# Seven half-size products in place of eight for the output product of the last batch

## The chip, the cores and the metric

The kernel runs on one core of one Trainium2 chip. The metric is the device time of one execution in microseconds. Before the change it is 569.72 us, the median of three runs (569.68 to 569.75).

## What is computed

Two stages follow one another. The first is an attention across channels for each of four batches of 5824 tokens with 256 channels; the second is a gated feed-forward layer over all 23296 tokens.

```
qn = q / (norm(q, over tokens) + 1e-6);  kn = k / (norm(k, over tokens) + 1e-6)
s  = kn^T @ qn / tau                      # 256 x 256 for each batch
a  = softmax(s, last axis)
x  = v @ a                                # tokens x 256
out = (((x @ w1) * (x @ w2)) @ w3) @ w_out    # d_ff = 1024, output tokens x 256, float32
```

Nothing nonlinear stands between `v @ a` and `w1`, `w2`, nor between `w3` and `w_out`. The kernel uses both facts: for each batch it folds `a` into `w1` and `w2` (called Wf, 256 x 1024 twice), and it multiplies `w3` by `w_out` once (called W_sb, 1024 x 256). What remains for each token is v times Wf twice, an elementwise product, and that product times W_sb.

## The kernel before, in words

A batch has 45 blocks of 128 tokens and 64 tokens left over. The main loop runs over the batch b (4), the chunk c (12) and the step j (8). Chunks 0 to 10 hold 512 tokens each; chunk 11 holds 128 tokens and the 64 left over, 192 columns. Step j stands for 128 of the 1024 hidden columns.

One step does this. `emit_ab` (L476) issues four matmuls, two for `a` and two for `b`, each 128 hidden columns by 512 tokens, into two tiles of PSUM; four such tiles exist, so TensorE can be two pairs ahead. ScalarE copies `a` to SBUF as bf16 (L482), and VectorE multiplies it by `b` (L497, or L487 in chunk 11). The result, `ab`, is put on the list `pend`. Then `emit_out` takes the oldest entries of `pend`, as long as more than a lag of two stand there, and issues their part of the output product (L521): for each of four blocks of 128 tokens, the block of `ab` is the stationary operand and row block j of W_sb (256 columns) is streamed. After the eighth step of a chunk the two PSUM tiles of its output go to SBUF, one through ScalarE (L542) and one through VectorE (L543), and a transfer on SyncE's queue writes 512 tokens out (L544).

Everything else, that is the scores of the next batch (L192, L189, L201), its softmax and its folding (L363 to L372), and the loads, is placed between these steps by an agenda: `at(t, cost, fn)` enters a piece with a due time, a running clock adds the modelled TensorE time of what was issued, and `run_due` issues all that is due. The order of instructions on each engine is the order of issue; no scheduler changes it. In the last batch no scores are computed, so TensorE has only the steps, and it has weight loads that overlap with the matmuls.

In the last batch the lag grows from 2 to 5 over chunk 10 and is 5 in chunk 11, so that the last matmuls wait for nothing. After the loop the five entries left are issued, tokens left over first.

Tiles come from pools with named tags: `q` (5 buffers), `k` (6) and `v` (3) for loaded inputs; `sq` and `o_sb` for temporaries; in PSUM `ab` (4), `out` (3) and `G` (1)[...].

Of the kernel before, what the change touches and what calls it, by code (L numbers as in the profile page):

```python
# [12 lines left out]
F32 = DT.float32  # L13
BF16 = DT.bfloat16

P = 128
PIECE = 8
LAG = 2
LAG_END = 5
IN_BUFS = {"q": 5, "k": 6, "v": 3}  # L20
MM_COL = 1.0 / 2400.0
MM_FIX = 0.0025
# [3 lines left out]
def kernel(  # L26
# [12 lines left out]
    nc = tc.nc  # L39

    B, N, C = q.shape
    T, D = out.shape
# [8 lines left out]
    FT = F // P  # L51
    NT = N // P
# [5 lines left out]
    NCH = NT // 4 + 1  # L58
# [6 lines left out]
    in_pool = ctx.enter_context(tc.tile_pool(name="in_pool", bufs=1))  # L65
# [375 lines left out]
    def at(t, cost, fn):  # L441
        seq[0] += 1
        agenda.append((t, seq[0], cost, fn))
# [26 lines left out]
    def emit_ab(b, c, j):  # L470
        n = chunk_cols(c)
        tiles = []
        for w in range(2):
            t = psum.tile([P, 512], F32, tag="ab", name=f"{'ab'[w]}_{b}_{c}_{j}", bufs=4)
            for ct in range(CT):
                nc.tensor.matmul(  # L476
                    t[:, :n], lhsT=Wf[b][:, ct, w, j * P : (j + 1) * P], rhs=rhs_of(b, c, ct),
                    start=(ct == 0), stop=(ct == CT - 1),
                )
            tiles.append(t)  # L480
        a_sb = work.tile([P, 512], BF16, tag="a_sb", name=f"as_{b}_{c}_{j}", bufs=4)
        nc.scalar.copy(a_sb[:, :n], tiles[0][:, :n])  # L482
        if c == NCH - 1:
            if b % 2 == 0 and j == 0:
                lefts[b // 2] = work.tile([P, FT, 2, P + LEFT], BF16, tag="left", name=f"left_{b}", bufs=1)
            both = lefts[b // 2][:, j, b % 2, :]
            nc.vector.tensor_mul(both, a_sb[:, :n], tiles[1][:, :n])  # L487
            ab = both[:, :P] if b % 2 == 0 else both[:, LEFT:]
        else:
            if b == 0 and c < 2:  # L490

                if j % 4 == 0:
                    held[0] = in_pool.tile([P, 4, 512], BF16, tag="q", name=f"abq_{c}_{j}", bufs=IN_BUFS["q"])
                ab = held[0][:, j % 4, :]
            else:
                ab = work.tile([P, 512], BF16, tag="ab_sb", name=f"abs_{b}_{c}_{j}", bufs=8 * NDEF + 2)
            nc.vector.tensor_mul(ab, a_sb, tiles[1])  # L497
        pend.append((b, c, j, ab))
        last_ab[0] = ab
        clock[0] += 4 * (n * MM_COL + MM_FIX)  # L500

    def emit_out(b, c, j, ab, only=None):

        small = c == NCH - 1
        if small:
            lhs = [ab[:, :P]]
            if b % 2 == 1:
                lhs.append(lefts[b // 2][:, j, :, :].rearrange("p b t -> p (b t)")[:, P : P + 2 * LEFT])
        else:
            lhs = [ab[:, i * P : (i + 1) * P] for i in range(4)]  # L510
        if j == 0:
            out_tiles[b, c] = [
                psum.tile([P, 2, D], F32, tag="out", name=f"o_{b}_{c}_{h}", bufs=3)
                for h in range(len(lhs) if small else 2)
            ]
        tl = out_tiles[b, c]
        for s, lhsT in reversed(list(enumerate(lhs))) if small else enumerate(lhs):
            if only is not None and s != only:
                continue
            h, o = (s, 0) if small else divmod(s, 2)  # L520
            nc.tensor.matmul(  # L521
                tl[h][:, o, :], lhsT=lhsT, rhs=W_sb[:, j, :],
                start=(j == 0 and o == 0), stop=(j == FT - 1 and (small or o == 1)),
                skip_group_check=True,
            )
        clock[0] += len(lhs) * (D * MM_COL + MM_FIX)
        if j == FT - 1:
            o = work.tile([P, 4, D], F32, tag="o_sb", name=f"osb_{b}_{c}", bufs=3)
            rows = out[b * N : b * N + NT * P, :].rearrange("(p i) c -> p i c", i=NT)
            if small:  # L530
                if b % 2 == 1 and only != 0:
                    o2 = work.tile([P, D], F32, tag="kr", name=f"oleft_{b}", bufs=1)
                    nc.vector.tensor_copy(o2, tl[1][:, 0, :])
                    for m in (b - 1, b):
                        k = (m - b + 1) * LEFT
                        nc.sync.dma_start(out=out[m * N + NT * P : (m + 1) * N, :], in_=o2[k : k + LEFT, :])
                if only != 1:
                    nc.scalar.copy(o[:, 0, :], tl[0][:, 0, :])
                    other = nc.scalar if b == B - 1 else nc.sync
                    other.dma_start(out=rows[:, NT - 1, :], in_=o[:, 0, :])  # L540
            else:
                nc.scalar.copy(o[:, 0:2, :], tl[0])  # L542
                nc.vector.tensor_copy(o[:, 2:4, :], tl[1])  # L543
                nc.sync.dma_start(out=rows[:, 4 * c : 4 * c + 4, :], in_=o)  # L544
            if only is None:
                del out_tiles[b, c]
# [119 lines left out]
    def make_agenda(b):  # L666
        agenda.clear()
        clock[0] = 0.0
        n = b + 1
        if b == 0:  # L670
            at(0.5, 0.87, soft0[5])
            for i in range(4):
                at((1.7, 2.6, 3.5, 3.9)[i], 0.43, soft0[7 + i])
            at(0.0, 0.0, load_library)
            at(4.6, 0.5, lambda: transpose_half_on_pe(0, 0, 1, False))
            at(7.0, 0.5, lambda: transpose_half_on_pe(0, 1, 0, True))
            at(8.0, 0.5, lambda: transpose_half_on_pe(0, 1, 1, False))
            at(15.0, 0.0, transpose_w3)
            at(15.0, 0.0, lambda: transpose_piece(0, 2))
            for jt in range(FT):  # L680
                at(27.5 + 1.2 * jt, 0.87, lambda jt=jt: w_unit(jt))
            moves = [("qk", 1, 0, 29.0), ("v", 0, 3, 30.0), ("v", 0, 4, 30.5), ("qk", 1, 1, 44.0), ("qk", 1, 2, 45.0)]
            moves += [("qk", 1, 3, 53.0), ("qk", 1, 4, 55.0), ("v", 0, 5, 61.0), ("qk", 1, 5, 73.0)]
            moves += [("v", 1, 0, 88.0), ("v", 1, 1, 98.0), ("v", 1, 2, 120.0), ("qk", 2, 0, 130.0)]
            t0, t1 = 54.0, 113.0
        else:
            moves = [("v", b, 3, 1.0), ("qk", n, 1, 10.0), ("qk", n, 2, 17.0), ("v", b, 4, 26.0), ("qk", n, 3, 38.0)]
            moves += [("v", b, 5, 46.0), ("qk", n, 4, 58.0), ("qk", n, 5, 66.0)]
            moves += [("v", n, 0, 76.0), ("v", n, 1, 86.0), ("v", n, 2, 96.0), ("qk", n + 1, 0, 108.0)]
            moves = [m for m in moves if m[1] < B]  # L690
            t0, t1 = 16.0, 98.0

        before = (0, 2) if b == 0 else None
        for nm, m, pi, t in moves:
            if before is not None and not (nm == "v" and before == (m, pi - 1) == (0, 3)):
                at(t, 0.0, lambda w=before: hold(vTs[w[0]][1][:1, 0, :1] if w[1] == NP_ - 1 else vTs[w[0]][0][:1, w[1] * PIECE, 0, :1]))
            at(t, 0.0, gate)
            if nm == "qk":
                at(t, 0.0, lambda m=m, pi=pi: load_qk(m, pi))
                before = None  # L700
            else:
                at(t, 0.0, lambda m=m, pi=pi: load_piece("v", m, pi))
                at(t + 4.0, 0.0, lambda m=m, pi=pi: transpose_piece(m, pi))
                before = (m, pi)
        if n == B:
            agenda.sort()
            return
        units = score_units(n)
        for i, (cst, fn) in enumerate(units):
            at(t0 + (t1 - t0) * i / len(units), cst, fn)  # L710
        soft = soft_units(n)
        for cst, t, fn in soft:
            at(t1 + 1.0 + t, cst, fn)
        agenda.sort()

    for b in range(B):
        make_agenda(b)
        for c in range(NCH):
            for j in range(FT):
                run_due()  # L720
                emit_ab(b, c, j)
                npop = 0
                lag = LAG
                if b == B - 1 and c >= NCH - 2:
                    lag = LAG_END if c == NCH - 1 else LAG + (LAG_END - LAG) * (j + 1) // FT
                while w_ready[0] and len(pend) > lag and npop < 2:
                    emit_out(*pend.pop(0))
                    npop += 1
                    run_due()
        run_due(1e9)  # L730
# [39 lines left out]
```

## Time and profile before

The table gives the busy time of each engine over the span of the profiled execution (567.7 us), and of the last batch's full chunks alone, from 446 to 557 us.

| engine | whole span | 446 to 557 us (111 us) |
|---|---|---|
| TensorE, matmuls | 557.6 us (98%) | 111.0 us |
| TensorE, weight loads | 355.4 us (63%) | 66.5 us |
| VectorE | 375.4 us (66%) | 65.6 us |
| ScalarE | 338.7 us (60%) | 56.9 us |
| GpSimd | 77.9 us (14%) | 3.0 us |

How to read it: a matmul's record runs from its start to the modelled end of its pipeline, so successive records overlap, and what a group costs is the difference of the starts of two groups, not the length in the record. In the same way the records of VectorE and ScalarE are a little longer than the distance between two operations that follow one another without a wait. The granted TensorE clock is full over the span. A gap on an engine that is not the bound costs nothing by itself.

### The profile page before, as it was taken

To read this page: it belongs to the slowest core of one execution; us is meant where nothing else is said; L and a number is where in the kernel's file an instruction comes from. 1 tells how busy PE (TensorE), PEld (TensorE's weight loads), DVE (VectorE), ACT (ScalarE), POOL (GpSimd) and SP (SyncE) were. 2 spreads that over 40 slices of the span, in tenths; PEclk is the share of its full clock that TensorE was granted. 3 is DMA by queue.
4 is the path that set the end of the run, shared out by engine and by line. 5 is a ranking of instruction groups with operands and counts; after the bars stand their busy time and mean duration, and the time that the engine had idled before them with its cause. 6 is when DMAs were issued, how large, how long until landed. Compare 5 with 4: busy or idle time off the path is not lost.

```text
span 567.7 us, 10095 instructions
## 1 busy us (share of the span) xinstructions
PE 557.6 (98%) x3755; PEld 355.4 (63%) x3755; DVE 375.4 (66%) x581; ACT 338.7 (60%) x627; POOL 77.9 (14%) x163
## 2 busy tenths in 40 slices
PE   8799999999999999999999999999999999999997
PEld 5664566776656666666656566666655655665655
DVE  1047645888966577888766668787876665565564
ACT  1057536777766577777675567777765554454453
POOL 4260013120111111121210101030120000000000
PEclk9999999999999999999999999999999999999999
DMA  9999989978455796595661595765740325221011
GB/s 213 211 182 209 173 171 237 226 164 192 115 142 121 143 192 148 90 193 123 145 149 75 97 219 117 155 120 121 185 112 39 85 74 149 64 68 71 38 70 61
DMA packets 75104, 77.45 MB, mean 136 GB/s; under 512 B 54192, under 2 KB 58800, under 8 KB 75056
## 3 DMA queue, kind: packets, MB, share of 16 engines
q0 software_dynamic: 15760, 38.93, 39.3%
q1 hardware_dynamic: 59008, 37.23, 22.0%
q10 hardware_dynamic: 288, 0.66, 0.4%
q8 instruction: 29, 0.48, 0.3%
q14 instruction: 19, 0.16, 0.1%
HBM read 78.91 MB, written 23.86 MB: 181 GB/s over the span
## 4 chain that ended last, share of the span: by engine, by line
PE 93%; DMA 5%; ACT 1%; POOL 0%; issue 0%; DVE 0%; ACTq 0%; POOLq 0%
PE o L521 28%; PE b L476 28%; PE a L476 28%; PE G L192 5%; DMA k<-in_k_dram 5%; PE fold L363 2%; PE w L649 1%; ACT kr L283 0%; PE quarter L389 0%; POOL k L111 0%; POOL q L111 0%; PE sqk L225 0%; PE row L271 0%; ACT e L322 0%; ACT Wf L398 0%
## 5 line engine op out<-in xcount | busy, mean ns | idle before, releaser
L497 DVE TENSOR_TENSOR abs<-as,b 128x512 bf16<-128x512 bf16 x336 | 230.6, 687 | 143.9 <-ACT as L482 131.4
L482 ACT CAST as<-a 128x512 bf16<-128x512 f32 (+1 forms) x384 | 215.9, 562 | 170.4 <-DVE abs L497 84.7
L476 PEld LDWEIGHTS <-Wf 128*128 128x128 bf16 x1536 | 149.0, 98 | 102.3 <-ACT Wf L398 0.6
L476 PE MATMUL a<-vT,Wf 128*128 128x512 bf16 x704 | 209.6, 379 | 0.4 <-ACT Wf L398 0.4
L476 PE MATMUL b<-vT,Wf 128*128 128x512 bf16 x704 | 209.6, 379 | 0.0
L521 PE MATMUL o<-W_sb,abs 128*128 128x256 bf16 x1344 | 201.5, 273 | 0.0
L521 PEld LDWEIGHTS <-abs 128*128 128x128 bf16 x1344 | 131.2, 98 | 79.8 <-issue 0.2
L201 DVE TENSOR_TENSOR acc<-acc,sq 128x1024 f32<-128x1024 f32 x66 | 80.4, 1219 | 0.6 <-ACT sq L189 0.6
L192 PE MATMUL G<-k,q 128*128 128x256 bf16 x276 | 49.8, 273 | 0.0
L189 ACT ACTIVATE sq<-q 128x512 f32<-128x512 bf16 x66 | 41.8, 633 | 0.0
L189 ACT ACTIVATE sq<-k 128x512 f32<-128x512 bf16 x66 | 41.5, 629 | 0.0
L464 POOL COPY gate_t<-abs 1x1 bf16<-1x1 bf16 x39 | 10.5, 269 | 171.7 <-DVE abs L497 168.8
L543 DVE COPY osb<-o 128x512 f32<-128x512 f32 x44 | 30.1, 685 | 0.9 <-PE o L521 0.9
L192 PEld LDWEIGHTS <-q 128*128 128x128 bf16 x276 | 27.0, 98 | 3.1
L542 ACT COPY osb<-o 128x512 f32<-128x512 f32 x44 | 25.8, 586 | 4.1 <-PE o L521 2.1
L468 POOL COPY gate_t<-vT 1x1 bf16<-1x1 bf16 x16 | 3.1, 193 | 158.8 <-DMA vT<-v 158.8
L111 POOL DMA_DIRECT2D q<-in_q_dram x28 | 15.1, 540 | 12.5 <-DMA k<-in_k_dram 5.5
L370 ACT ACTIVATE Wf<-fold,rs 128x512 bf16<-128x512 f32 x15 | 10.3, 687 | 10.9 <-PE fold L363 8.7
L283 ACT ACTIVATE kr<-row 128x256 f32<-128x256 f32 x1 | 0.4, 383 | 26.1 <-PE row L271 26.1
L363 PE MATMUL fold<-w,e 128*128 128x512 bf16 x56 | 15.0, 379 | 0.0
L487 DVE TENSOR_TENSOR left<-as,b 128x192 bf16<-128x192 bf16 x32 | 11.3, 354 | 5.1 <-ACT as L482 2.7
L497 DVE TENSOR_TENSOR abq<-as,b 128x512 bf16<-128x512 bf16 x16 | 10.8, 686 | 5.0 <-ACT as L482 4.5
(98 smaller groups left out, 242.3 us busy)
## 6 DMA issues: line engine op xcount, KB each, us to landing
out_dram<-osb SPq DMA_DIRECT2D x44, 512.0 KB, 3.3
k<-in_k_dram POOLq DMA_DIRECT2D x19, 512.0 KB, 8.3
v<-in_v_dram POOLq DMA_DIRECT2D x19, 512.0 KB, 5.2
q<-in_q_dram POOLq DMA_DIRECT2D x18, 512.0 KB, 5.8
w_wout<-in_moe_w_dram POOLq DMA_DIRECT2D x1, 2048.0 KB, 22.7
k<-in_k_dram POOLq DMA_DIRECT2D x4, 320.0 KB, 8.8
v<-in_v_dram POOLq DMA_DIRECT2D x4, 320.0 KB, 4.9
q<-in_q_dram POOLq DMA_DIRECT2D x3, 320.0 KB, 4.1
```

The lines of the kernel that those rows point to most:

```text
L111: nc.gpsimd.dma_start(out=pieces[nm, n, pi][:, lo:hi, :], in_=qk_main[nm, n][0][:, pi * PIECE + lo : pi * PIECE + hi, :])
L189: nc.scalar.activation(out=dst[:, :, part, :], in_=src[:, o : o + 2, :], func=AF.Square)
L192: nc.tensor.matmul(G[:, ct, :], lhsT=qt[:, i, ct * P : (ct + 1) * P], rhs=kt[:, i, :], start=(pr == 0 and part == 0 and ct == 0), stop=(pr ...
L201: nc.vector.tensor_add(accs[n], accs[n], sqs[0])
L363: nc.tensor.matmul(m, lhsT=st["e"][:, c2, c1 * P : (c1 + 1) * P], rhs=w12[:, c2, w, lo:hi], start=(c2 == 0), stop=(c2 == CT - 1),)
L476: nc.tensor.matmul(t[:, :n], lhsT=Wf[b][:, ct, w, j * P : (j + 1) * P], rhs=rhs_of(b, c, ct), start=(ct == 0), stop=(ct == CT - 1),)
L482: nc.scalar.copy(a_sb[:, :n], tiles[0][:, :n])
L487: nc.vector.tensor_mul(both, a_sb[:, :n], tiles[1][:, :n])
L497: nc.vector.tensor_mul(ab, a_sb, tiles[1])
L521: nc.tensor.matmul(tl[h][:, o, :], lhsT=lhsT, rhs=W_sb[:, j, :], start=(j == 0 and o == 0), stop=(j == FT - 1 and (small or o == 1)), skip ...
L542: nc.scalar.copy(o[:, 0:2, :], tl[0])
L543: nc.vector.tensor_copy(o[:, 2:4, :], tl[1])
```

## The change

The output of a chunk is C = A B, with A = `ab` (512 tokens x 1024) and B = W_sb (1024 x 256). In the eleven full chunks of the last batch all three axes are halved: A11, A12, A21, A22 are 256 tokens x 512, B11 to B22 are 512 x 128. In place of the eight products of halves there are seven, of sums and differences (the scheme of Strassen in Winograd's form):

```
S1 = A21 + A22   S2 = S1 - A11   S3 = A11 - A21   S4 = A12 - S2
T1 = B12 - B11   T2 = B22 - T1   T3 = B22 - B12   T4 = B21 - T2
P1 = A11 B11  P2 = A12 B21  P3 = S4 B22  P4 = A22 T4  P5 = S1 T1  P6 = S2 T2  P7 = S3 T3
C11 = P1 + P2                     C12 = P1 + P6 + P5 + P3
C21 = P1 + P6 + P7 + P4           C22 = P1 + P6 + P7 + P5
```

(T4 is used with the sign that makes C21 a plain sum.) It is meant to take matmul columns off TensorE. T1 to T4 are computed once, near the end of batch 2 (`combine_weights`), and kept as bf16. For each chunk VectorE computes S1, S2 and S4 and GpSimd computes S3. TensorE accumulates in three PSUM banks: bank A takes P1, then P6, P7 and P4 on top of it, and ScalarE copies its content after each; bank B takes P2; bank C takes P5 and later P3. VectorE joins these into the quarters of the output tile. The nine pieces `p1, p2, p5, p6, rest (S4), p7, c22, p4, p3` go on `pend` when a chunk's eighth step is issued, and one is taken after each step (p4 and p3 together), so the products of a chunk run during the next chunk. `ab` now lies in two tiles of four steps each, from the tags `q` and `k`.

```diff
-            if b == 0 and c < 2:
+            if fast(b, c):
+                if j % 4 == 0:
+                    nm = "qk"[j // 4]
+                    halves[j // 4] = in_pool.tile([P, 4, 512], BF16, tag=nm, name=f"abh_{c}_{j}", bufs=IN_BUFS[nm])
+                ab = halves[j // 4][:, j % 4, :]
+            elif b == 0 and c < 2:
...
-        pend.append((b, c, j, ab))
         last_ab[0] = ab
+        if not fast(b, c):
+            pend.append((b, c, j, ab))
+        elif j == FT - 1:
+            pend.extend(seven_products(b, c, *halves))
...
+    def combine_weights():
+        T = in_pool.tile([P, 4, 4, P], BF16, tag="q", name="wcomb", bufs=IN_BUFS["q"])
+        f = work.tile([P, 2, 4, P], F32, tag="sq", name="wcomb_f", bufs=2)
...
+        nc.vector.tensor_sub(f[:, 0], b12, b11)
+        nc.vector.tensor_sub(f[:, 1], b22, f[:, 0])
+        nc.scalar.copy(T[:, 0], f[:, 0])
+        nc.scalar.copy(T[:, 1], f[:, 1])
+        nc.vector.tensor_sub(T[:, 2], b22, b12)
+        nc.vector.tensor_sub(T[:, 3], b21, f[:, 1])
...
+        def product(nm, a, w, first, last):
+            for j in range(4):
+                for i in range(2):
+                    nc.tensor.matmul(
+                        st[nm][:, i, :], lhsT=a[:, j, i * P : (i + 1) * P], rhs=w[j],
+                        start=(first and j == 0 and i == 0), stop=(j == 3),
+                        skip_group_check=True,
+                    )
...
+        def p1():
...
+            nc.vector.tensor_add(s1, a21, a22)
+            nc.gpsimd.tensor_sub(s3, a11, a21)
+            bank("A")
+            product("A", a11, w1, True, False)
+            nc.scalar.copy(keep(0), st["A"])
+        def p2():
+            nc.vector.tensor_sub(s2, s1, a11)
+            bank("B")
+            product("B", a12, w21, True, True)
+            nc.vector.tensor_add(quarter(0, 0), st["B"], keep(0))
+        def p5():
+            bank("C")
+            product("C", s1, t1, True, False)
+        def p6():
+            product("A", s2, t2, False, False)
+            nc.scalar.copy(keep(1), st["A"])
+        def rest():
+            nc.vector.tensor_sub(s4, a12, s2)
+        def p7():
+            product("A", s3, t3, False, False)
+            nc.scalar.copy(keep(2), st["A"])
+        def c22():
+            nc.vector.tensor_add(quarter(1, 1), st["C"], keep(2))
+        def p4():
+            product("A", a22, t4, False, True)
+            nc.scalar.copy(quarter(1, 0), st["A"])
+        def p3():
+            product("C", s4, w22, False, True)
+            nc.vector.tensor_add(quarter(0, 1), st["C"], keep(1))
...
+        return [p1, p2, p5, p6, rest, p7, c22, p4, p3]
...
+        if n == B - 1:
+            at(126.0, 0.0, combine_weights)
...
-                lag = LAG
-                if b == B - 1 and c >= NCH - 2:
-                    lag = LAG_END if c == NCH - 1 else LAG + (LAG_END - LAG) * (j + 1) // FT
-                while w_ready[0] and len(pend) > lag and npop < 2:
-                    emit_out(*pend.pop(0))
+                lag, most = LAG, 2
+                if b == B - 1:
+                    lag = 0
+                    if c < NCH - 1:
+                        most = 1
+                while w_ready[0] and len(pend) > lag and npop < most:
+                    if b == B - 1 and c == NCH - 1 and not callable(pend[0]) and pend[0][2] > j - LAG_END + npop:
+                        break
+                    out_step()
```

More of the change, by code (lines that the diff above doesn't have):

```diff
@@ L497, in emit_ab, with fast @@
             nc.vector.tensor_mul(ab, a_sb, tiles[1])
-        pend.append((b, c, j, ab))
         last_ab[0] = ab
+        if not fast(b, c):
+            pend.append((b, c, j, ab))
+        elif j == FT - 1:
+            pend.extend(seven_products(b, c, *halves))
         clock[0] += 4 * (n * MM_COL + MM_FIX)
+    def fast(b, c):
+        return b == B - 1 and c < NCH - 1
+    halves = [None, None]
+    shared = {}
+    def combine_weights():
+        T = in_pool.tile([P, 4, 4, P], BF16, tag="q", name="wcomb", bufs=IN_BUFS["q"])
+        f = work.tile([P, 2, 4, P], F32, tag="sq", name="wcomb_f", bufs=2)
+        b11, b12 = W_sb[:, 0:4, :P], W_sb[:, 0:4, P:]
+        b21, b22 = W_sb[:, 4:8, :P], W_sb[:, 4:8, P:]
+        nc.vector.tensor_sub(f[:, 0], b12, b11)
[4 more added lines that the diff above has]
+        nc.vector.tensor_sub(T[:, 3], b21, f[:, 1])
+        shared["T"] = T
+        shared["S12"] = in_pool.tile([P, 2, 4, 2 * P], BF16, tag="k", name="S12", bufs=IN_BUFS["k"])
+        shared["S34"] = in_pool.tile([P, 2, 4, 2 * P], BF16, tag="k", name="S34", bufs=IN_BUFS["k"])
@@ new lines, in seven_products, with bank, quarter, keep @@
+    def seven_products(b, c, k1, k2):
+        T, S12, S34 = shared["T"], shared["S12"], shared["S34"]
+        a11, a21 = k1[:, :, : 2 * P], k1[:, :, 2 * P :]
+        a12, a22 = k2[:, :, : 2 * P], k2[:, :, 2 * P :]
+        s1, s2, s3, s4 = S12[:, 0], S12[:, 1], S34[:, 0], S34[:, 1]
+        w1 = [W_sb[:, j, :P] for j in range(4)]
+        w21 = [W_sb[:, 4 + j, :P] for j in range(4)]
+        w22 = [W_sb[:, 4 + j, P:] for j in range(4)]
+        t1, t2, t3, t4 = ([T[:, i, j, :] for j in range(4)] for i in range(4))
+        st = {}
+        def bank(nm):
+            st[nm] = psum.tile([P, 2, P], F32, tag="out", name=f"prod{nm}_{c}", bufs=3)
+        def product(nm, a, w, first, last):
[6 more added lines that the diff above has]
+                    )
+            clock[0] += 8 * (P * MM_COL + MM_FIX)
+        def quarter(r, d):
+            return st["o"][:, 2 * r : 2 * r + 2, d * P : (d + 1) * P]
+        def keep(i):
+            return st["keep"][:, i, :, :]
+        def p1():
+            st["keep"] = work.tile([P, 3, 2, P], F32, tag="sq", name=f"keep_{c}", bufs=2)
+            st["o"] = work.tile([P, 4, D], F32, tag="o_sb", name=f"osb_{b}_{c}", bufs=3)
+            nc.vector.tensor_add(s1, a21, a22)
[27 more added lines that the diff above has]
+            nc.vector.tensor_add(quarter(0, 1), st["C"], keep(1))
+            rows = out[b * N : b * N + NT * P, :].rearrange("(p i) c -> p i c", i=NT)
+            nc.sync.dma_start(out=rows[:, 4 * c : 4 * c + 4, :], in_=st["o"])
+        return [p1, p2, p5, p6, rest, p7, c22, p4, p3]
@@ L502, in emit_out, with out_step @@
+    def out_step():
+        u = pend.pop(0)
+        if not callable(u):
+            emit_out(*u)
+            return
+        u()
+        name = u.__name__
+        if name == "p4" and len(pend) > 1:
+            pend.pop(0)()
     def emit_out(b, c, j, ab, only=None):
```

## The prediction

> **What bounds the kernel now.** I read the page first: busy times, then the chain that ended last.
>
> ```profile
> PE 557.6 (98%) x3755; PEld 355.4 (63%) x3755; DVE 375.4 (66%) x581; ACT 338.7 (60%) x627; POOL 77.9 (14%) x163
> ...
> PE 93%; DMA 5%; ACT 1%; POOL 0%; issue 0%; DVE 0%; ACTq 0%; POOLq 0%
> PE o L521 28%; PE b L476 28%; PE a L476 28%; PE G L192 5%; DMA k<-in_k_dram 5%; PE fold L363 2%; PE w L649 1%; ACT kr L283 0%; PE quarter L389 0%; POOL k L111 0%; POOL q L111 0%; PE sqk L225 0%; PE row L271 0%; ACT e L322 0%; ACT Wf L398 0%
> ```
>
> TensorE is the bound, and the output product (o, L521) is 28% of the chain. So time taken out of L521 in the last batch leaves the span, unless TensorE gets a wait in its place. Next the timeline of TensorE inside the last batch (start, length, group):
>
> ```profile
> 500.43 0.60 PE L521 MATMUL o<-W_sb,abs 128*128 128x256 bf16 x4
> 500.86 0.59 PE L476 MATMUL a<-vT,Wf 128*128 128x512 bf16 x2
> 501.30 0.60 PE L476 MATMUL b<-vT,Wf 128*128 128x512 bf16 x2
> 501.73 0.60 PE L521 MATMUL o<-W_sb,abs 128*128 128x256 bf16 x4
> ```
>
> From start to start, a pair of a or b takes 0.433 us, four output matmuls 0.433, a step 1.300; no idle is noted. Then the timeline of all engines around a chunk's end, for how VectorE and ScalarE follow:
>
> ```profile
> 548.96 0.59 PE L476 MATMUL a<-vT,Wf 128*128 128x512 bf16 x2
> 549.40 0.59 PE L476 MATMUL b<-vT,Wf 128*128 128x512 bf16 x2
> 549.60 0.59 ACT L482 CAST as<-a 128x512 bf16<-128x512 f32 x1 [0.71 <-DVE abs L497]
> 550.21 0.69 DVE L497 TENSOR_TENSOR abs<-as,b 128x512 bf16<-128x512 bf16 x1 [0.61 <-PE o L521]
> ...
> 550.82 0.68 DVE L543 COPY osb<-o 128x512 f32<-128x512 f32 x1
> ```
>
> The copy of a starts 0.64 after a's first matmul, the multiply 1.25 after it and ends at 1.94. On a full VectorE the next operation starts 0.61 after a multiply of 0.69. VectorE is idle 0.61 of each 1.30. Last, the early 128-column matmuls, each with its own weights, and the by-form rows for the small operations:
>
> ```profile
> 13.03 1.07 PE L225 MATMUL sqq<-q 128*128 128x128 bf16 x16 [0.73 <-DMA q<-in_q_dram]
> 13.93 1.91 PE L237 MATMUL G<-k,q 128*128 128x256 bf16 x16
> ```
>
> ```profile
> L538 ACT COPY osb<-o 128x256 f32<-128x256 f32 x4 | 1.5, 372 | 1.2 <-PE o L521 1.2
> ...
> L317 DVE TENSOR_TENSOR s<-G,kr 128x256 f32<-128x256 f32 x8 | 3.2, 416 | 0.2 <-ACT kr L283 0.2
> ```
>
> **What the Trainium skill says.** "TensorE: Matmul & The Clock Gate", section on 56 against 53.3 ns: a warm 128-column matmul starts every 55.6 ns. The trace agrees: 16 of L225 in 0.90 us, 56.3 ns each, weight loads hidden. "VectorE: DVE Perf Modes", the perf-mode tier table: a two-input operation on 16-bit data wholly in SBUF runs at two elements a cycle, any PSUM operand keeps it at one; no row of before shows the former. "SBUF — State Buffer", section "Who interferes with whom": a VectorE operation with two SBUF inputs and a GpSimd operation that reads SBUF lock each other out for a whole instruction; no row of before has that pair.
>
> **The change part by part.**
>
> *Fewer columns.* Per full chunk before: 32 matmuls of 128x256 in 8 groups of 0.433 = 3.467 us. After: 7 products of 8 matmuls of 128x128, 56 x 56.3 ns = 3.150. Saved 0.316 a chunk, 11 chunks: **-3.48 us**. The eighth saved is mostly there (9.1% of the product's time, not 12.5%, for the fixed part of a small matmul).
>
> *Combined weights (once, batch 2).* The order of instructions puts four VectorE operations of 128x512 between the multiplies of chunk 10, steps 6 and 7, and two ScalarE copies ahead of step 7's cast. The timeline of before there:
>
> ```profile
> 438.60 0.69 DVE L497 TENSOR_TENSOR abs<-as,b 128x512 bf16<-128x512 bf16 x1 [0.61 <-ACT as L482]
> 439.28 0.58 ACT L482 CAST as<-a 128x512 bf16<-128x512 f32 x1 [0.72 <-DVE abs L497]
> 439.90 0.69 DVE L497 TENSOR_TENSOR abs<-as,b 128x512 bf16<-128x512 bf16 x1 [0.61 <-ACT as L482]
> 440.71 0.33 PE L476 MATMUL a<-vTt,Wf 128*128 128x192 bf16 x2
> 440.88 0.33 PE L476 MATMUL b<-vTt,Wf 128*128 128x192 bf16 x2
> ```
>
> First difference 439.21 to 439.90; the second needs it, to about 440.62; the ScalarE copy of the second starts at 440.65, holds the engine some 0.5, so step 7's cast runs 441.15 to 441.73 instead of from 439.28, and its multiply to 442.44. The b matmuls of 440.88 need the PSUM tile that this multiply frees: they start near 442.46. **+1.6 us** of TensorE idle. Nothing hides it: TensorE is only two PSUM pairs ahead. Bounds: 1.0 if only the a tile counted, 1.9 with slower dependent steps.
>
> *Per-chunk sums.* VectorE gets s1, s2, s4 (128x1024 bf16) and three adds of 128x256 from PSUM. The adds cost 0.416 each (L317), 0.335 when back to back. A sum is bounded by 0.69 (two elements a cycle, the length of a 512-element multiply) and 1.22 (the f32 row of 128x1024, L201, 1219 ns). I take 0.69, by the skill's table. VectorE then has 8 x 0.61 + 3 x 0.61 + 3 x 0.335 = 7.7 us in a chunk of 10.1: not the bound. The two copies of L542 and L543 go; ScalarE gets four of 372 ns (L538) for one of 586, which its idle time takes. GpSimd's s3: an estimate from "GPSIMD Engine Reference", section 3.1 (4497 ns for 2048 elements of f32), is 2.2 us for 1024. It may start only when p7 of the chunk before has read its tile, and p7 of its own chunk comes 10 us later: hidden. By then s4 is nearly over and the next s1 is 4 us off, so I see no clash on the port.
>
> *Where TensorE waits within a chunk.* Its order in steady state: ab0 p1 ab1 p2 ab2 p5 ab3 p6 ab4 ab5 p7 ab6 ab7 p4 p3, with ab = 0.867 and a product 0.450. I followed each engine's queue with the durations above. The sums s1 and s2 are ready 0.9 us and 0.8 us before p5 and p6; b7 waits for multiply 5, which s4 delays, and has 0.3 left. One wait is not covered: p3 accumulates into bank C, so it must wait until c22 has read C. Counted from the start of ab6: multiply 6 starts at 1.25, c22 at 1.25 + 0.61 = 1.86 and ends at 2.28. TensorE is at p3 at 2 x 0.867 + 0.45 = 2.18. With 0.03 for the signal p3 idles 0.12 us. Behind it on TensorE stands all the next chunk. Nine chunks (chunk 0 has an ab between p4 and p3, chunk 10 is the tail): **+1.1 us**; bounds 0 and 2.7 (0.3 a chunk).
>
> *Tail.* Chunk 11's steps are short (four matmuls of 192 columns, 0.33 us) with two products each, so the chains show. From its start at 0: s1 can start only at 0.99, behind the last multiply, an add and the first small multiply; it ends at 1.68 where p5 could start at 1.56; s2 ends at 2.40, p6 idles 0.27; the copies "keep" between p6 and p7 and between p7 and p4 (0.16 + 0.03 + 0.37, against 0.33 of ab) idle 0.25 each. Sum 0.91, against 0.21 of idle in before's tail (6.75 us for 6.54 of matmuls): **+0.7 us**, bounds 0.3 and 1.2. What follows the last matmul (copy, output transfer) is as before.
>
> *At no cost:* the lag of zero in the last batch only moves output work from chunk 0 into the following steps; in the six steps of ab alone (0.867 each) multiply j ends at 1.94 and b of step j+2 comes at 2.17. The operand buffers in the q and k tags are free, as no scores are computed in the last batch. Output bytes are the same.
>
> Sum: -3.48 + 1.6 + 1.1 + 0.7 = -0.1; 569.72 - 0.1 = **569.6 us**.
>
> **The rivals.**
>
> *B, the gain arrives.* If c22 comes early enough for p3 and half of the tail's waits vanish: -3.48 + 1.6 + 0.35 = -1.5, **568.2 us**. For it: 0.12 us is the difference of two sums of 2.2. Against it: every term is a measured start difference.
>
> *C, VectorE's sums at one element a cycle* (1.22, 1.14 in a queue). Then s2 ends at 4.83 and p6 wants 4.82, s4 delays multiply 5 past b7 (0.2), multiply 6 slips and c22 with it: about 0.37 a chunk in place of 0.12, +2.5 over ten chunks: **572.2 us**, slower than before. For it: no operation of this kind in the trace. Against it: the skill's table.
>
> *D, a wait I don't see*, such as s3 holding the port over s1 or s4, or weight loads that show between products. p5 has 0.9 of slack, so 1.3 us of lock-out or more would cost 0.4 a chunk or more: 569.6 + 4.4 = **574 us**, more if all of s3 counts. For it: three engines now exchange tiles at each step. Against it: the order above keeps s3 off the sums.
>
> **How the numbers follow.** Forecast 43%, B 22%, C 15%, D 20%. Faster by over 0.2% (1.14 us) is B, 0.22; within it the forecast, 0.43; slower C and D, 0.35. The range is B's 568.2 less 0.3 for the lower bound of the combining cost, to C's 572.2 plus 1.0 for the unknown wait per chunk: 567.9 to 573.2. Outside are the longer half of D and little of B.
>
> **What would show it.** In the profile of after: product groups of eight at 0.45 us; TensorE idle per chunk near 0.12 before p3, released by VectorE's c22; a gap near 1.6 us at the end of batch 2 before b of chunk 11; sums of 0.69 on VectorE; about 0.9 us of gaps in the last chunk. I am wrong if sums take 1.2, if p5, p6 or b wait in each chunk, if s3's time overlaps a late s1 or s4, or if p3 does not wait.

## The result and the profile after

The changed kernel takes 573.34 us (median of four runs, 573.22 to 576.53), against 569.74 us for the kernel before in the same session. The medians differ by 3.6 us. The ratio is 1.0076, 95% interval 1.0052 to 1.0100: slower. (It is a ratio of means, and the one run at 576.53 raises it; that of the medians is 1.0063.) The forecast was 569.6 us, the upper end of its range 573.2.

First the page of after, the busy times and the chain that ended last:

```profile
PE 557.6 (98%) x4012; PEld 356.9 (62%) x4019; DVE 404.5 (71%) x640; ACT 350.0 (61%) x662; POOL 102.7 (18%) x174
...
PE 89%; DMA 5%; DVE 3%; ACT 1%; POOL 1%; issue 1%; ACTq 0%; DVEq 0%; POOLq 0%
```

TensorE's part of the chain went from 93% to 89%, and VectorE, ScalarE and GpSimd stand in it now. TensorE is still the bound, but it waits. (Its busy time is the same as before, 557.6 us, although columns were taken away: a record runs on to the modelled end of the pipeline, 0.61 us for a group that costs 0.45, so a wait of up to 0.16 us behind each group counts as busy. The starts show it.) Next the waits of TensorE from 430 us on (for whom, us in total, times, longest):

```profile
PE prodC L550 <- DVE S L566: 1.6, 2, 1.0
PE prodA L550 <- POOL S L567: 1.6, 1, 1.6
PE a L476 <- ACT as L482: 0.9, 1, 0.9
PE prodC L550 <- DVE osb L594: 0.3, 1, 0.3
PE o L638 <- DVE abs L502: 0.2, 1, 0.2
```

L550 is the product helper, L566 is s1 on VectorE, L567 is s3 on GpSimd, L594 is c22. The third and the fifth row are the combining of weights and the fourth belongs to the tail; both were foreseen. The first two rows were not: three waits, in three of eleven chunks. The view counts only part of an idle stretch, and drops short ones, so I measure from starts.

**A chunk without trouble.** The timeline around a chunk's last steps (start, length, engine, line, operation, and in brackets the idle time before):

```profile
515.07 0.68 DVE L502 TENSOR_TENSOR abh<-as,b 128x512 bf16<-128x512 bf16 x1
515.09 2.12 POOL L567 TENSOR_TENSOR S<-abh 128x1024 bf16<-128x1024 bf16 x1 [8.06 <-PE prodA L550]
...
516.52 0.61 PE L550 MATMUL prodA<-wcomb,abh 128*128 128x128 bf16 x8
516.64 0.42 DVE L594 TENSOR_TENSOR osb<-prodC,keep 128x256 f32<-128x256 f32 x1
...
517.11 0.61 PE L550 MATMUL prodC<-W_sb,S 128*128 128x128 bf16 x8
```

p4 starts at 516.52 and p3 at 517.11, 0.59 later in place of 0.45: p3 waits 0.14 us for c22, as foreseen (0.12). The whole chunk takes 10.18 us from start to start (first a at 507.38, the next at 517.56), against 10.40 before (eight steps of 1.30). s3 and a multiply start together at 515.07 and neither is longer for it.

**A chunk with trouble.** The same view at the start of the fifth chunk's products:

```profile
496.24 0.18 POOL L464 COPY gate_t<-abh 1x1 bf16<-1x1 bf16 x1 [10.39 <-DVE abh L502]
...
496.76 0.57 POOL L108 DMA_DIRECT2D v<-in_v_dram  x1 [0.34 <-issue]
...
497.90 2.15 POOL L567 TENSOR_TENSOR S<-abh 128x1024 bf16<-128x1024 bf16 x1
497.93 2.68 DVE L566 TENSOR_TENSOR S<-abh,abh 128x1024 bf16<-128x1024 bf16 x1
...
500.67 0.62 PE L550 MATMUL prodC<-wcomb,S 128*128 128x128 bf16 x8 [1.01 <-DVE S L566]
```

GpSimd sat idle for 10.39 us on a "gate" (L464). A gate is a copy of one element of the newest `ab`, put on GpSimd's queue ahead of a load of v so that the load is not issued too early; it waits for a multiply on VectorE. Behind it stand two load issues, and behind these s3, which therefore starts beside s1. s1, normally 0.68 us, takes 2.68: it ends at 500.61, 0.56 after s3's end. p5 waits for s1, and TensorE loses 1.18 us (prodB at 498.19, then a and b, 0.43 each, would have let it start at 499.49). In the third chunk s1 takes 2.36 us for the same reason and costs 0.79:

```profile
476.37 2.13 POOL L567 TENSOR_TENSOR S<-abh 128x1024 bf16<-128x1024 bf16 x1
476.71 2.36 DVE L566 TENSOR_TENSOR S<-abh,abh 128x1024 bf16<-128x1024 bf16 x1
```

**The first chunk.** GpSimd, and the product that reads s3:

```profile
448.76 0.18 POOL L464 COPY gate_t<-abh 1x1 bf16<-1x1 bf16 x1 [32.16 <-DVE abh L502]
449.28 0.55 POOL L111 DMA_DIRECT2D v<-in_v_dram  x1 [0.33 <-issue]
458.57 2.11 POOL L567 TENSOR_TENSOR S<-abh 128x1024 bf16<-128x1024 bf16 x1 [8.74 <-DVE abh L502]
...
460.73 0.62 PE L550 MATMUL prodA<-wcomb,S 128*128 128x128 bf16 x8 [1.62 <-POOL S L567]
```

s3 starts at 458.57. The bracket blames a multiply, but the last multiply into the tile that s3 reads ended at 450.47. What lies in between is an instruction that, by its name, sets GpSimd up anew: the list of what stands on s3's line has

```profile
L567 POOLq MODIFY_POOL_CONFIG  x2: 37/37/37, 449.9 to 449.9; - x2
```

I call the time behind it the preparation. p7 reads s3, so it waits until s3 ends at 460.68, starts at 460.73, and TensorE loses 1.78 us. s4 beside this s3 takes 2.15 us in place of 0.68, but nothing waits for that: the loss of this chunk is the lateness of s3 alone.

| Term | predicted, us | measured in the trace, us |
|---|---|---|
| fewer columns, 11 chunks | -3.5 | -4.0 (10.40 less 10.03, the 10.18 without p3's wait) |
| combining the weights | +1.6 | +1.48 |
| p3 behind c22, nine chunks | +1.1 | +1.3 |
| tail | +0.7 | +1.3 |
| late s3, chunks 0, 2, 4 | 0 | +3.75 (1.78 + 0.79 + 1.18) |
| sum | -0.1 | +3.8 (profiled span 571.5 against 567.7) |

### The profile page after: what moved, and what is told of

It is laid out like the page before. It is cut to its first block, busy times and chain, and to the rows that moved or that the text cites. A ratio compares the mean times of both kernels' runs of the same rounds, so it can differ in the third digit from the quotient of the medians.

```text
span 571.5 us, 10735 instructions
## 1 busy us (share of the span) xinstructions
PE 557.6 (98%) x4012; PEld 356.9 (62%) x4019; DVE 404.5 (71%) x640; ACT 350.0 (61%) x662; POOL 102.7 (18%) x174
## 4 chain that ended last, share of the span: by engine, by line
PE 89%; DMA 5%; DVE 3%; ACT 1%; POOL 1%; issue 1%; ACTq 0%; DVEq 0%; POOLq 0%
PE a L476 27%; PE b L476 27%; PE o L638 21%; PE G L192 5%; DMA k<-in_k_dram 5%; PE prodA L550 3%; PE fold L363 2%; PE prodC L550 2%; PE w L766 1%; DVE S L566 1%; ACT as L482 1%; PE prodB L550 1%; POOL S L567 0%; DVE abs L502 0%; DVE abh L502 0%
## 5 line engine op out<-in xcount | busy, mean ns | idle before, releaser
L502 DVE TENSOR_TENSOR abs<-as,b 128x512 bf16<-128x512 bf16 x248 | 169.8, 686 | 97.3 <-ACT as L482 91.0
L476 PEld LDWEIGHTS <-Wf 128*128 128x128 bf16 x1536 | 146.3, 98 | 106.4 <-issue 1.5
L638 PE MATMUL o<-W_sb,abs 128*128 128x256 bf16 x992 | 148.7, 273 | 0.2 <-DVE abs L502 0.2
L638 PEld LDWEIGHTS <-abs 128*128 128x128 bf16 x992 | 96.9, 98 | 58.6 <-DVE abs L502 0.4
L502 DVE TENSOR_TENSOR abh<-as,b 128x512 bf16<-128x512 bf16 x88 | 60.0, 684 | 20.4 <-ACT as L482 20.4
L567 POOL TENSOR_TENSOR S<-abh 128x1024 bf16<-128x1024 bf16 x11 | 23.4, 2127 | 59.6 <-PE prodA L550 50.8
L550 PEld LDWEIGHTS <-S 128*128 128x128 bf16 x352 | 22.9, 98 | 13.6 <-DVE S L566 2.8
L464 POOL COPY gate_t<-abs 1x1 bf16<-1x1 bf16 x36 | 10.0, 278 | 113.8 <-DVE abs L502 110.9
L660 DVE COPY osb<-o 128x512 f32<-128x512 f32 x33 | 22.6, 685 | 1.0 <-PE o L638 1.0
L550 PEld LDWEIGHTS <-abh 128*128 128x128 bf16 x264 | 17.4, 98 | 7.3 <-issue 0.3
L659 ACT COPY osb<-o 128x512 f32<-128x512 f32 x33 | 19.4, 587 | 3.7 <-PE o L638 2.5
L370 ACT ACTIVATE Wf<-fold,rs 128x512 bf16<-128x512 f32 x15 | 10.3, 688 | 10.9 <-PE fold L363 7.9
```

The source lines that it names most:

```text
L476: nc.tensor.matmul(t[:, :n], lhsT=Wf[b][:, ct, w, j * P : (j + 1) * P], rhs=rhs_of(b, c, ct), start=(ct == 0), stop=(ct == CT - 1),)
L550: nc.tensor.matmul(st[nm][:, i, :], lhsT=a[:, j, i * P : (i + 1) * P], rhs=w[j], start=(first and j == 0 and i == 0), stop=(j == 3), skip_ ...
L567: nc.gpsimd.tensor_sub(s3, a11, a21)
L638: nc.tensor.matmul(tl[h][:, o, :], lhsT=lhsT, rhs=W_sb[:, j, :], start=(j == 0 and o == 0), stop=(j == FT - 1 and (small or o == 1)), skip ...
```

## The experiments

My theory: the miss is s3's place on GpSimd's queue, where it comes late behind gates and a preparation of GpSimd and then collides with VectorE's sums. The rivals: three engines exchanging tiles cost this wherever s3 runs; or only one of the two causes counts. All ratios are to the kernel before, run on the same chip.

**s3 on VectorE, at the same place.**

```diff
-            nc.gpsimd.tensor_sub(s3, a11, a21)
+            nc.vector.tensor_sub(s3, a11, a21)
```

> The changed kernel with s3 computed by VectorE instead of GpSimd, at the same place in the order; nothing else differs. Theory (s3 on GpSimd is late in chunks 0, 2 and 4, because a gate, transfers to issue or the switch to another GpSimd program stand ahead of it in its queue, and then locks s1 or s4 out): the three TensorE waits of 1.8, 0.8 and 1.2 us go, and VectorE takes eleven more operations of 0.61 us in its idle time, so 573.3 - 3.7 = 569.6 us. Rival (VectorE is simply too full in the first chunks, or s1 is late for another reason): more work on VectorE makes those waits longer, 573.3 or more.

569.88 us, ratio 1.0008 (1.0000 to 1.0017). The late waits are gone. All four sums take 0.685 us on VectorE, and its extra 7.5 us over the batch lengthen only one wait of TensorE that shows: p6 in the last chunk waits 0.75 us for s2, by its starts, where it waited 0.28. So the miss is s3 on GpSimd. It does not say what makes it late.

**The preparation earlier.** GpSimd gets one small subtraction in batch 2, long before it is needed; gates and s3 stay.

```diff
+    def load_tensor_library():
+        m = work.tile([P, 1], F32, tag="lib", name="lib2", bufs=1)
+        nc.gpsimd.tensor_sub(m, ones_f, eps_t)
...
+            at(112.0, 0.0, load_tensor_library)
```

> The changed kernel with one more GpSimd subtraction of 128x1, issued in batch 2 after the all-reduce, so that whatever GpSimd has to prepare for its first subtraction is done before s3 of chunk 0. Theory: the 8.7 us between the last load and s3 of chunk 0 are this preparation, not a wait for a multiply (the tile that it reads was complete 7 us before); s3 of chunk 0 then starts near 451 us, s4 and p7 of chunk 0 wait for nothing: 573.3 - 1.8 = 571.5 us. Rival (s3 waits for VectorE as the trace's releaser says): s3 stays at 458 us, 573.3 us.

571.44 us, ratio 1.0031 (1.0019 to 1.0044). GpSimd at the small subtraction and in the first chunk:

```profile
423.61 0.18 POOL L786 TENSOR_TENSOR lib<-ones_f,eps_t 128x1 f32<-128x1 f32 x1 [7.13 <-issue]
448.64 0.18 POOL L464 COPY gate_t<-abh 1x1 bf16<-1x1 bf16 x1 [24.85 <-DVE abh L502]
449.15 0.74 POOL L111 DMA_DIRECT2D v<-in_v_dram  x1 [0.33 <-issue]
450.44 2.12 POOL L567 TENSOR_TENSOR S<-abh 128x1024 bf16<-128x1024 bf16 x1 [0.55 <-DVE abh L502]
```

Gate and load are where they were, and s3 follows 0.55 us after the load, 8 us earlier than in after. So the 8.7 us were the preparation, not the multiply that the bracket named. In this kernel it shows at the small subtraction, which starts at 423.61, 7.1 us after GpSimd's all-reduce ended; MODIFY_POOL_CONFIG stands there, at 416.4, and no more at s3.

The preparation shows in a third place. Before has a small all-reduce early on, and it starts at once. In after it starts 9.47 us late:

```profile
37.77 0.42 POOL L663 PARTITION_ALL_REDUCE lib<-ones_f  x1
...
47.04 0.40 POOL L780 PARTITION_ALL_REDUCE lib<-ones_f  x1 [9.47 <-issue]
```

(The first line is from before, the second from after.) It is late, by 9.1 to 10.3 us, in every kernel here with a subtraction on GpSimd, and at once in the kernels without one: before, s3 on VectorE, and the fill below. I read this as the two needing different set-ups, so that each has to be prepared once both stand in a kernel. Early on it costs nothing, as GpSimd has nothing to do then.

The two other waits remain, as the theory said (1.4 us in the list of waits, s1 up to 2.67 us).

**No gates in the last batch.**

```diff
-            at(t, 0.0, gate)
+            if n < B:
+                at(t, 0.0, gate)
```

> The changed kernel without the gates (the GpSimd copies that hold the loads of v back until a multiply is done) in the last batch. Theory: s3 of chunks 2 and 4 no longer stands behind a gate and the issue of a load, starts right after p7 of the chunk before, and s1 keeps its 0.68 us; the wait of chunk 0 stays: 573.3 - 2.0 = 571.3 us. Rival (the gate is not what delays it, or the loads that start earlier get in the way): 573.3 or more.

569.49 us, ratio 0.9998 (0.9990 to 1.0007). I had expected 571.3, with the first chunk still late. GpSimd shows why it isn't:

```profile
416.39 0.55 POOL L111 DMA_DIRECT2D v<-in_v_dram  x1
450.47 2.13 POOL L567 TENSOR_TENSOR S<-abh 128x1024 bf16<-128x1024 bf16 x1 [33.52 <-DVE abh L502]
```

With no gate on the queue GpSimd issues the load at 416.39, right after the all-reduce, reaches the preparation at 417.0, and then waits for the first tile. So the gate caused all three late starts, the first by holding the preparation back for over 30 us. With the run before this splits the miss: 573.34 - 571.44 = 1.9 us for the first chunk, 571.44 - 569.49 = 1.95 for the two others (trace: 1.78 and 1.97). The first of these is the less exact: the two times are from different sessions, in which before itself took 569.74 and 569.42 us, and 1.6 us remains when each is taken against its own.

**A fill in place of s3.** To ask what holds s1: GpSimd writes a constant to the same tile and reads nothing. The subtraction is left out, so the seventh product is of other numbers.

```diff
-            nc.gpsimd.tensor_sub(s3, a11, a21)
+            nc.gpsimd.memset(s3, 0.25)
```

> The changed kernel with s3 replaced by a fill of the same tile with a constant on GpSimd (the subtraction of S3 is left out, so the seventh product is of other numbers); queue and place are the same. It writes SBUF and reads none. If the lock is on SBUF reads that VectorE and GpSimd share, s1 of chunks 2 and 4 takes 0.68 us although the fill runs at that time, and the time falls by 2 us or more (chunk 0 too, if the fill needs no preparation): 569.6 to 571.4 us. If any GpSimd operation that overlaps holds VectorE up, s1 there stays longer than 0.68 by as long as the fill lasts.

569.46 us (a single run). The fifth chunk:

```profile
495.17 0.97 POOL L567 MEMSET S<- 128x1024 bf16 x1
495.21 0.68 DVE L566 TENSOR_TENSOR S<-abh,abh 128x1024 bf16<-128x1024 bf16 x1
```

The gates are there, the fill is as late as s3 was, and the whole of s1 lies inside it; s1 keeps its 0.68. In the third chunk they overlap by 0.38 us, with the same outcome. So GpSimd's being at work, or writing, does not stop s1. What is left is its reading, or something else that sets a subtraction apart from a fill; another GpSimd operation that reads was not run. Reading is what the Trainium skill names, in "SBUF — State Buffer", section "Who interferes with whom": a VectorE operation with two SBUF inputs contends with a GpSimd instruction that reads SBUF, not with one that only writes. The traces here agree in each of the three collisions (the sum ends 0.55 to 0.57 us after s3), in the fill, and in the multiplies, which have one input in PSUM and stay at 0.68 beside s3. That page's words on a hold "for the whole instruction" stand under another kind of VectorE instruction; these traces show it for a sum with two SBUF inputs. The fill was also under way at 449.7 in the first chunk, with no preparation ahead of it.

**The foreseen waits, taken away one by one.** The next kernels are without gates. First the combining of weights, cut into four steps laid 2 to 3 us apart, earlier in batch 2 (the part that makes the tiles for the sums stays where it was):

```diff
-            at(126.0, 0.0, combine_weights)
+            for i in range(4):
+                at((104.0, 107.2, 109.8, 112.2)[i], 0.0, lambda i=i: combine_step(i))
+            at(126.0, 0.0, combine_tiles)
```

> The kernel without gates in the last batch, with the four VectorE operations and two ScalarE copies that combine the weights issued one at a time in four different steps of batch 2, some 20 to 30 us earlier, after the all-reduce, instead of all between two steps of chunk 10. If the 1.5 us of TensorE waits at the end of batch 2 come from their being issued in one go: 569.5 - 1.5 = 568.0 us. If the work as such costs the time, wherever it stands: 569.5 us.

568.14 us, ratio 0.9976 (0.9968 to 0.9984), 1.35 less than without gates alone: the 1.6 of the prediction was of the right size. Of the waits of TensorE from 430 us on, only one line is left:

```profile
PE prodC L558 <- DVE osb L602: 0.3, 1, 0.3
```

Then c22 straight after p7's copy, one step earlier:

```diff
         def p7():
             product("A", s3, t3, False, False)
             nc.scalar.copy(keep(2), st["A"])
+            nc.vector.tensor_add(quarter(1, 1), st["C"], keep(2))
...
         def c22():
-            nc.vector.tensor_add(quarter(1, 1), st["C"], keep(2))
+            pass
```

> The kernel without gates in the last batch, with c22 issued on VectorE right after p7 instead of a step later (its inputs are ready then), so that p3 finds bank C read. If the 0.15 us in front of p3 in nine chunks and 0.5 us in the tail are the wait for c22: 569.5 - 1.8 = 567.7 us, and in each chunk p3 starts 0.45 after p4. If p3 waits for something else (s4, or the change from one bank to another): 569.5 us.

568.21 us, ratio 0.9978 (0.9970 to 0.9987): 1.3 less, where I expected 1.8. Its runs spread more widely (567.7 to 569.22), and the fastest of them reach the 1.8. A chunk now takes 10.03 us (p5 at 506.54 and 516.57), and c22 is done 0.87 before p3.

Both together:

> All three edits together: no gates in the last batch, weights combined in four steps, c22 right after p7. If the costs are separate they add: 569.5 - 1.5 - 1.8 = 566.2 us, faster than before the change by 3.2 us (0.6%). If one of them hides another, less than that: 567 us or more.

566.37 us, ratio 0.9946 (0.9931 to 0.9960). The costs add: c22 on top of the spread weights is worth 568.14 - 566.37 = 1.77 us, the 1.3 of nine chunks and 0.4 of the tail. The list of waits of TensorE from 430 us on is empty.

Last the tail, with one product after each short step in place of two:

```diff
-                    if c < NCH - 1:
-                        most = 1
+                    most = 3 if c == NCH - 1 and j == FT - 1 else 1
```

> The three edits and, in the last chunk of the last batch, one product after each short step instead of two, so that the sums and the copies between products have a step to run beside. TensorE's idle in the tail, 1.5 us in the changed kernel of which c22 was 0.5, falls to 0.3 or less: 566.2 - 0.8 = 565.4 us. If the output transfer of chunk 10, which then starts later, ends last: 566.2 us or more.

565.63 us, ratio 0.9932 (0.9915 to 0.9949), faster than both kernels. Against before it saves 3.85 us: nearly the whole -4.0 of the columns is there once nothing waits. One wait is left in the list, 0.2 us before a b.

## Why the prediction was wrong

**The step that failed** is the one on GpSimd's s3: "It may start only when p7 of the chunk before has read its tile, and p7 of its own chunk comes 10 us later: hidden. By then s4 is nearly over and the next s1 is 4 us off, so I see no clash on the port." It asks when s3's tile and buffer are ready. It does not ask what stands ahead of s3 on GpSimd's queue. There stood, in three chunks, a gate that waits for a late multiply, then one or two load issues, and in the first chunk a preparation of 8.7 us. GpSimd's row of before (3.0 us busy in the last batch) gave no warning, since a queue that waits is not busy; but GpSimd's timeline of before has the three gates, each after a long wait for a multiply:

```profile
447.36 0.18 POOL L464 COPY gate_t<-abs 1x1 bf16<-1x1 bf16 x1 [30.67 <-DVE abs L497]
...
471.73 0.18 POOL L464 COPY gate_t<-abs 1x1 bf16<-1x1 bf16 x1 [14.82 <-DVE abs L497]
...
491.29 0.18 POOL L464 COPY gate_t<-abs 1x1 bf16<-1x1 bf16 x1 [9.95 <-DVE abs L497]
```

Reading that one view would have shown where s3 would stand. In the eight other chunks the step held. What it had put at nothing measured 3.75 us.

Rival D named the mechanism, s3 over s1 or s4, and its slack for p5 was right: with 0.9 us of slack, s1 longer by 1.68 and 2.00 us would cost 0.78 and 1.10, and cost 0.79 and 1.18. It was about half of the miss: the 1.78 us of the first chunk came from s3's lateness, not from the clash. D took it as a cost in every chunk, 574 us; the late s3 came in three, at 573.3. That the two totals are close is chance. The range ended at 573.2 because the longer half of D was left out.

The preparation could have been suspected too, though not from before's trace, where the first all-reduce follows MODIFY_POOL_CONFIG at once (37.77 and 37.7). The Trainium skill, "GPSIMD Engine Reference", section 2.1, tells of a program load of about 6 us at the first call to newly loaded code, counted from MODIFY_POOL_CONFIG, with no instruction in the profile for it. The traces here have 7.1 us and 8.7 us ahead of the first subtraction; the measurements decide. That the wait is this load is argued from the page and the place, and what the difference between the two consists of is open.

**Sizes.** Fewer columns: 0.37 a chunk, not 0.316. I took the output group as 0.433, rounded from two starts; eight steps of 1.30 less the 0.863 of a pair step make it 0.437, and a step in after is 0.863 where I had 0.867. Combining: 1.48 for 1.6. The delayed multiply ended where the sum had it (442.38 for 442.44), but what waited was different: a 1.09 us for the cast, and the output product that reads the multiply's result 0.33, while b, on which the forecast put all of it, lost 0.05. p3: 0.147 for 0.12; "the difference of two sums of 2.2" was right to within 0.03. Tail: 1.3 for 0.7. Waits of p5, p6 and the two copies were there (0.17, 0.28, 0.29, 0.28), but p3 stood another 0.50, since c22 is behind the multiply of the left-over tokens on VectorE; I had not followed that. Three of the prediction's small sums do not follow from the figures beside them, and none decided the outcome: the two copies in the tail come to 0.23 each and not 0.25, C to 572.1 and not 572.2, and the lower end of the range takes off 0.3 for the combining where its bound of 1.0 takes off 0.6.

**What held.** Sums of 0.684 us on VectorE, which ends rival C with its 1.22; s3's length (2.12 for 2.2); VectorE not the bound; no wait in the steps without a product. Without the failed step the forecast's 569.6 us has its counterpart in two runs, s3 on VectorE (569.88) and no gates (569.49). That they come so near is luck in part: -0.5 us for the columns and -0.1 for the combining nearly cancel +0.2 for p3 and +0.6 for the tail. B's 568.2 was reached only with two further changes (no gates, c22 early).

## What to carry to other kernels

When work is put on an engine that looks idle, read its queue and not its busy share: list every instruction ahead of the new one, what each waits for, and whether the engine must be set up anew. A sum on VectorE with both inputs in SBUF and an operation on GpSimd that reads SBUF should be ordered so that they can't meet, or put on one engine: here the fourth sum cost 569.88 - 569.49 = 0.4 us on VectorE, and on GpSimd behind its gates 3.5 us more. A saving of a few us on the bound is kept only if each new wait is under its slack; list those waits with their sizes first, since each could here be removed by moving a few instructions.

## What the runs showed of the hardware

- A subtraction 128x1024 of bf16 takes 2.12 us on GpSimd and 0.684 us on VectorE with both inputs in SBUF. In the three places of after where they met, the VectorE sum started second and ended 0.55 to 0.57 us after the GpSimd one: 2.15, 2.36 and 2.68 us for 0.68. What happens when GpSimd comes second was not seen.
- GpSimd needed 7.1 and 8.7 us before its first subtraction after an all-reduce, and in kernels that have such a subtraction 9.1 to 10.3 us before their first all-reduce, which starts at once in the others. The profile shows no busy time for it, and the releaser it names can be another one. Moving the one before the subtraction to an idle place took one instruction.
- A constant fill 128x1024 of bf16 on GpSimd takes 0.95 to 0.97 us, needs no such preparation (in the first chunk the load ahead of it takes from 449.20 to 449.75, and it starts at 449.74), and does not hold up a VectorE sum (0.68 us inside it).
